# Reading the moving operand of float32r products as two interleaved halves

## The chip, the cores and the metric

One Trainium2 chip, one core. The metric is the device time of one launch in microseconds. TensorE, VectorE, ScalarE, GpSimd and SyncE appear in the profile as PE (with PEld for its weight loads), DVE, ACT, POOL and SP.

## What is computed

The reference, cut to what matters:

```python
x: (4, 12480, 128); inducing: (32, 128); w_in: (128, 2048); w_out: (2048, 128)
def mab(q, kv):
    s = scale * (q @ kv.transpose(0, 2, 1))
    a = softmax(s)
    return a @ kv
h   = mab(inducing for each batch, x)      # 32 summary rows per batch
y   = mab(x, h).reshape(49920, 128)        # every token attends to its batch's 32 rows
g   = y @ w_in
out = maximum(0.01 * g, g) @ w_out
```

All of it is float32.

## The kernel before

A token's attention output is `a @ h`, with `a` 32 wide, so the kernel never forms it: for each batch it makes `hw = h @ w_in` once (32 x 2048) and multiplies the 32-wide weights `a` by that. The leaky part is split as `0.99 * relu(g) + 0.01 * g`. The second half is linear and becomes one more 32-row product (`linear_part`, and the `LINEAR` branch of `products`), so that the main work is relu and two products.

Tokens are taken in tiles of 512 columns (`TOK`); two tiles are 384 wide, put together from two batches' remainders of 192. Every tile goes through 16 slices `f` of the hidden dimension. To keep float32 accuracy at the speed of float32r, each operand is split into a high and a low float32r part, and a product is three passes: high times high, low times high, high times low.

For one tile and slice:
- the first product, three passes with 32 contracted rows (`quarter`, L1147 to 1151, operands `A4` and `hw`), into a PSUM bank `ph`;
- the split of relu(`ph`) into `ghi` and `glo`. On the near way ACT writes `ghi` (`high`, L1135) and DVE takes `max(ph, 0) - ghi` as `glo` (`low`, L1138). On the far way ACT copies relu(`ph`) to `g` in SBUF, and POOL makes `ghi` (L1417, or L1111) and `glo` (L1419, or L1113) from it. POOL has no part in PSUM here;
- the second product, with 128 contracted rows. In the main part it is cut into four groups of 32 rows of the array that run side by side: each row group makes its three passes of 32 rows into its own bank, again through `quarter`. So a tile and slice costs 3 + 4 x 3 = 15 quarter passes, and four quarter passes run at once in the four row groups. Only the first two tiles and the last use the whole array for the second product (`ffn_second`, L1180).

After slice 15 the four banks of a tile are gathered: ACT copies banks 0 and 2 to SBUF (`copied`, L1445), DVE adds banks 1 and 3 (`summed`, L1451), POOL adds the two sums (`joined`, L1462), DVE transposes blocks (`store`, L1205) and SP sends the result out. The three tiles with one bank are transposed straight from PSUM.

The order of all instructions on all engines is written out when the program is built. A planner in the kernel (`turn_over`, `option`, `go`, `relu`, `best`, `clustered`) keeps a clock for each engine and each row group and issues next what can start first by these clocks. Its costs are constants: `QUARTER` for a 512-column pass, `RELU`, `LOW`, `FAR_HIGH`, `FAR_LOW` and so on for the other steps (`spent`, `on_rows`, `on_array`), and `SLOT` for the pace of a tile and slice, by which `relu` decides for the far way only if POOL would be done in time. The attention work of later batches (L395, L482, L575, L817) runs between the products in gangs that `clustered` lets in, held back by `IDLE`, `HURRY`, `WAITING` and the list `WAITS`. The engines keep semaphores between them, so a wrong clock makes a wait and not a wrong result.

The moving operand of every product above is read in order, one column after the other, from SBUF:

```python
nc.tensor.matmul(dst, w[32 * r : 32 * r + 32], x[32 * r : 32 * r + 32], ...)
```

Of the kernel before, what the change touches and what calls it, by code (L numbers as in the profile page):

```python
# [9 lines left out]
F32 = mybir.dt.float32  # L10
# [9 lines left out]
def induced_attention_then_leaky_ffn(  # L20
# [34 lines left out]
    while N - base >= 4 * TOK:  # L55
# [29 lines left out]
    A4_BUFS = 3  # L85
    XR = 7
    GB = 10
    SLOT = 868.0
    QUARTER = 232.6
    SIGNAL, TO_ARRAY, TO_POOL = 35.0, 150.0, 160.0  # L90
    DRAINED = 200.0
    TURNED, LOADED = 100.0, 100.0
    LANDED = 3800.0
    RELU, LOW, COPIED, ADDED, BLOCKS = 599.0, 690.0, 587.0, 691.0, 702.0
    FAR_HIGH, FAR_LOW, FAR_SUM = 613.0, 1310.0, 1297.0
    SETTLED = 75.0
    EARLY, PREFER, YIELDING, PATIENCE = 250.0, 0.0, 200.0, 6000.0
    IDLE, HURRY, APART, TAIL, WAITING, SOON = 600.0, 3000.0, 60000.0, 5000.0, 3000.0, 3000.0
    NEAR, BANKS, AT_ONCE, BEHIND = 3, 1, 2000.0, 1200.0
    LINEAR = NF - 3  # L100
    SPREAD = 80.0
    BEGUN = 3
    WAITS = [
# [3 lines left out]
    ]  # L107
    AHEAD = 100.0
    PACE, STOCK = 41250.0, 4
# [35 lines left out]
    def spent(engine, ns, *after):  # L145
        if not timing[0]:
            return 0.0
        signal = TO_POOL if engine == POOL else SIGNAL
        clock[engine] = max([clock[engine], now[0], *(a + signal for a in after)]) + ns
        return clock[engine]  # L150

    def on_array(kind, ns, *after):
        if not timing[0]:
# [943 lines left out]
    def split_first(ph, t, f, at):  # L1097

        _, n = spans(t)
        ghi = sb.tile([P, TOK], F32R, tag="ghi", name="ghi", bufs=GB)  # L1100
        glo = sb.tile([P, TOK], F32R, tag="glo", name="glo", bufs=GB)
        live[t, f] = (ghi, glo)
        start = max(clock[ACT], at + SIGNAL)
        if far_ends[-2:-1] <= [start] and max(clock[POOL], start + RELU) + FAR_HIGH + FAR_LOW < (
            max(clock[DVE], start + RELU) + LOW + BEHIND
        ):
            g = sb.tile([P, TOK], F32, tag="g", name="g", bufs=2)
            high(ph, g, n)
            at = spent(ACT, RELU, at)
            done(ph, at)  # L1110
            nc.gpsimd.tensor_copy(ghi[:, :n], g[:, :n])  # L1111
            high_of[t, f] = spent(POOL, FAR_HIGH, at)
            nc.gpsimd.tensor_tensor(  # L1113
                out=glo[:, :n], in0=g[:, :n], in1=ghi[:, :n].bitcast(F32), op=ALU.subtract
            )
            low_of[t, f] = spent(POOL, FAR_LOW) + SETTLED
            far_ends.append(low_of[t, f])
            return
        high(ph, ghi, n)
        high_of[t, f] = at = spent(ACT, RELU, at)  # L1120
        low(ph, ghi, glo, n)
        low_of[t, f] = at = spent(DVE, LOW, at)
        done(ph, at)
# [9 lines left out]
        return start + ns + DRAINED  # L1133

    def high(ph, ghi, n):  # L1135
        nc.scalar.activation(ghi[:, :n], ph[:, :n], AF.Relu)  # L1136

    def low(ph, ghi, glo, n):  # L1138
        nc.vector.scalar_tensor_tensor(  # L1139
            out=glo[:, :n],  # L1140
            in0=ph[:, :n],
            scalar=0.0,
            in1=ghi[:, :n].bitcast(F32),
            op0=ALU.max,
            op1=ALU.subtract,
        )

    def quarter(dst, w, x, r, start, stop):
        nc.tensor.matmul(  # L1149
            dst, w[32 * r : 32 * r + 32], x[32 * r : 32 * r + 32],  # L1150
            start=start, stop=stop, tile_position=(32 * r, 0),
        )

# [7 lines left out]
    def ffn_first(t, f):  # L1161

        n = spans(t)[1]
        ph = gen_ps("ph")
        for o, w, wt, a, k in first_products(t, f):
            quarter(ph[:, o : o + w], wt, a, f % 4, k == 0, k == 2)
            at = on_rows(f % 4, QUARTER * w / TOK, max(rows[f % 4], landed.get(("A", t), 0.0) + SIGNAL))
            if o + w == n:
                yield
        split_first(ph, t, f, at)  # L1170

    def ffn_second(t, f):

        parts, n = spans(t)
        ghi, glo = live.pop((t, f))
        if f == 0:
            accs[t] = bank("out")
        po = accs[t]
        for w, r in ((w_hi, ghi), (w_lo, ghi), (w_hi, glo)):
            nc.tensor.matmul(  # L1180
                po[:, :n], w[:, f, :], r[:, :n], start=(f == 0 and r is ghi and w is w_hi),
                stop=(t > 0 and f == NF - 1 and r is glo),
            )
            at = on_array("f", QUARTER * n / TOK, (high_of if r is ghi else low_of)[t, f])
        return at

    def linear_part(t):

        parts, n = spans(t)
        for b, o, w in parts:  # L1190
            for k in range(3):
                nc.tensor.matmul(
                    accs[t][:, o : o + w], hw[b][1 + k % 2][:M, TOK:], A4[t][:M, k // 2, o : o + w],
                    start=False, stop=(t == 0 and k == 2 and o + w == n), tile_position=(0, 0),
                )
                at = on_array("r", QUARTER * w / TOK)
        del A4[t]
        landed["A4"] = at
        return at

    def store(t, total, summed, at=0.0):
        _, n = spans(t)
        yield from new(DVE, at)
        osb = sb.tile([P, TOK], F32, tag="osb", name="osb", bufs=2)
        nc.vector.transpose(osb[:, :n], total[:, :n])  # L1205
        at = spent(DVE, BLOCKS, at)
        if summed:
            parts_used[0] -= 1
        else:
            done(total, at)  # L1210
        yield from old(HEAVY)
        o = 0
        for b, g, js in tiles[t]:
            base, J, K = GROUPS[g]
            n = 32 * K
            for j in js:
                yield from new(SP, at)
                row = b * N + base + j * 32 * K
                dst = out[row : row + n, :].rearrange("(r k) c -> r k c", k=K)
                for cb in range(NB):  # L1220

                    (nc.scalar if t == NT - 1 and cb % 2 else nc.sync).dma_start(
                        dst[:, :, 32 * cb : 32 * cb + 32],
                        osb[32 * cb : 32 * cb + 32, o : o + n].rearrange("p (k c) -> p k c", c=32),
                    )
                    spent(SP, 675.0, at)
                o += n
            yield from old()
# [40 lines left out]
    with tc.manual_schedule():  # L1269
# [131 lines left out]
        def relu(i, ph, ready):  # L1401
# [7 lines left out]
            if far_open[0] < 2 and left <= start and far <= wanted:  # L1409
                g = sb.tile([P, TOK], F32, tag="g", name="g", bufs=2)  # L1410
                high(ph, g, n)
                at = spent(ACT, RELU, ready)
                done(ph, at)
                far_open[0] += 1

                def on_pool():
                    nc.gpsimd.tensor_copy(ghi[:, :n], g[:, :n])  # L1417
                    high_at[i] = spent(POOL, FAR_HIGH, at)
                    nc.gpsimd.tensor_tensor(  # L1419
                        out=glo[:, :n], in0=g[:, :n], in1=ghi[:, :n].bitcast(F32), op=ALU.subtract  # L1420
                    )
                    low_at[i] = spent(POOL, FAR_LOW) + SETTLED
                    far_ends.append(low_at[i])
                    far_open[0] -= 1

                add(POOL, at, FAR_HIGH + FAR_LOW, on_pool)
                return
# [10 lines left out]
        def gather(t, r, ready):  # L1438
# [3 lines left out]
            def copied():  # L1442
                parts_used[0] += r == 0
                part = sb.tile([P, TOK], F32, tag="part", name="part", bufs=2)
                nc.scalar.copy(part[:, :n], po[:, :n])  # L1445
                parts_of[t, r] = part, spent(ACT, COPIED, ready)
                done(po, clock[ACT])

            def summed():
                part, at = parts_of[t, r - 1]  # L1450
                nc.vector.tensor_tensor(out=part[:, :n], in0=po[:, :n], in1=part[:, :n], op=ALU.add)  # L1451
                at = spent(DVE, ADDED, ready, at)
                parts_of[t, r] = part, at
                done(po, at)
                if r == 3:
                    add(POOL, at, FAR_SUM, joined, lambda: (t, 1) in parts_of)
# [70 lines left out]
        def go(r, kind, start):  # L1527
# [12 lines left out]
            if kind == "on":  # L1540
# [2 lines left out]
                _, n = spans(t)  # L1543
                o, w, wt, a, k = todo.pop(0)
                quarter(ph[:, o : o + w], wt, a, r, k == 0, k == 2)
                at = on_rows(r, QUARTER * w / TOK, start)
                if not todo:
                    running_first[r] = None
                    add(ACT, at, RELU, lambda: relu(i, ph, at))
# [10 lines left out]
                accs[t, r][:, o : o + width], w, x, r,  # L1560
                f == 0 and product_of[r] == 0, f == NF - 1 and last,
            )
            at = on_rows(r, QUARTER * width / TOK, start)
            product_of[r] += 1
            if last:
                product_of[r] = 0
# [169 lines left out]
```

## Time and profile before

| | us |
|---|---|
| median of 3 runs (1524.4 to 1525.05) | 1524.87 |
| span of the profiled execution, first to last instruction | 1523.1 |
| median less that span | 1.77 |
| PE busy / POOL busy | 1508.4 / 1363.5 |
| ACT busy / DVE busy | 1072.7 / 1029.2 |

Busy time is the time in which at least one instruction of the engine ran. Matmuls overlap, so a busy PE says only that it never stood still. The tables by line give, after the count, the group's busy time in us and the mean duration in ns of one instruction. In tables by stage every engine has its busy time and, in brackets, its count of instructions.

### The profile page before, as it was taken

Reading aid. Unit: us, or ns where it says so; the run is one execution under the profiler, and the core shown is the slowest. Engines: PE = TensorE matmul, PEld = TensorE weight load, DVE = VectorE, ACT = ScalarE, POOL = GpSimd, SP = SyncE. Lnnn points to the kernel's source line nnn. Section 1 sums busy time; section 2 is a strip of 40 time slices with the busy share of each in tenths; the row PEclk is TensorE's granted clock in tenths of the full one; section 3 lists DMA queues with packets and bytes.
Section 4 is the critical chain, followed back from the end, with each engine's and each line's share of the span. In section 5 each row is a group of like instructions: output and inputs, shape, how many; then the busy total and the mean of one; then the engine's idle time right before and its main releaser. Section 6 shows DMA issues by size and latency. Waiting matters only on the chain.

```text
span 1523.1 us, 60527 instructions
## 1 busy us (share of the span) xinstructions
PE 1508.4 (99%) x25207; PEld 1347.1 (88%) x25207; DVE 1029.2 (68%) x1811; ACT 1072.7 (70%) x1956; POOL 1363.5 (90%) x1435
## 2 busy tenths in 40 slices
PE   8999999999999999999999999999999999999998
PEld 5689989888899989888989999888899889999997
DVE  6867777666677777666677677666667666576564
ACT  6566777766777677776767777677777777777774
POOL 1478999999999999889989998999999999989997
PEclk9999999999999999999999999999999999999999
DMA  8155555443544454442644445342223223223231
GB/s 280 17 123 95 98 100 111 88 101 87 96 79 92 77 114 85 94 106 65 117 79 86 83 101 106 85 99 58 51 57 64 51 57 61 51 55 66 53 63 22
DMA packets 400706, 128.52 MB, mean 84 GB/s; under 512 B 373136, under 2 KB 375600, under 8 KB 400432
## 3 DMA queue, kind: packets, MB, share of 16 engines
q1 hardware_dynamic: 399328, 124.50, 39.3%
q8 instruction: 198, 3.24, 0.9%
q14 instruction: 76, 0.62, 0.1%
q10 hardware_dynamic: 1104, 0.15, 0.1%
HBM read 48.94 MB, written 25.56 MB: 49 GB/s over the span
## 4 chain that ended last, share of the span: by engine, by line
PE 97%; DVE 1%; ACT 1%; DMA 0%; issue 0%; POOL 0%; SPq 0%; DVEq 0%; ACTq 0%; POOLq 0%
PE bank L1149 89%; PE bank L395 3%; PE bank L1180 2%; PE bank L575 2%; PE bank L722 1%; DMA xr<-in_x_dram 0%; DVE glo L1139 0%; ACT xT L728 0%; ACT ghi L1136 0%; PE bank L817 0%; DVE cv_t L227 0%; PE bank L1055 0%; DVE sm L950 0%; SPq L700 0%; PE bank L482 0%
## 5 line engine op out<-in xcount | busy, mean ns | idle before, releaser
L1149 PE MATMUL bank<-ghi,w_hi 32*128 32x512 f32 (+1 forms) x6080 | 1182.5, 390 | 0.0
L1149 PE MATMUL bank<-ghi,w_lo 32*128 32x512 f32 (+1 forms) x6080 | 1180.4, 389 | 0.0
L1149 PE MATMUL bank<-glo,w_hi 32*128 32x512 f32 (+1 forms) x6080 | 1178.3, 389 | 0.0
L1149 PE MATMUL bank<-A,hwhi 32*128 32x512 f32 (+1 forms) x3394 | 1016.4, 387 | 0.2
L1139 DVE SCALAR_TENSOR_TENSOR glo<-bank,ghi 128x512 fp32r<-128x512 f32 (+1 forms) x948 | 632.1, 682 | 371.8 <-ACT ghi L1136 354.0
L1419 POOL TENSOR_TENSOR glo<-g,ghi 128x512 fp32r<-128x512 f32 (+1 forms) x611 | 789.0, 1291 | 48.9
L1149 PEld LDWEIGHTS bank<-ghi,w_hi 32*128 32x128 f32 x6080 | 757.2, 183 | 25.7 <-issue 1.4
L1149 PEld LDWEIGHTS bank<-ghi,w_lo 32*128 32x128 f32 x6080 | 752.8, 183 | 24.1 <-issue 1.6
L1149 PEld LDWEIGHTS bank<-glo,w_hi 32*128 32x128 f32 x6080 | 752.1, 183 | 24.1 <-issue 2.2
L1136 ACT ACTIVATE ghi<-bank 128x512 fp32r<-128x512 f32 (+1 forms) x948 | 552.9, 597 | 160.4 <-PE bank L1149 135.3
L1149 PE MATMUL bank<-A,hwlo 32*128 32x512 f32 (+1 forms) x1697 | 606.0, 385 | 0.0
L1149 PEld LDWEIGHTS bank<-A,hwhi 32*128 32x128 f32 x3394 | 552.3, 183 | 19.2 <-issue 2.4
L1136 ACT ACTIVATE g<-bank 128x512 f32<-128x512 f32 (+1 forms) x620 | 370.0, 598 | 217.8 <-PE bank L1149 194.1
L1417 POOL CAST ghi<-g 128x512 fp32r<-128x512 f32 (+1 forms) x611 | 374.0, 612 | 36.9 <-ACT g L1136 28.8
L1149 PEld LDWEIGHTS bank<-A,hwlo 32*128 32x128 f32 x1697 | 297.3, 183 | 6.4 <-issue 0.8
L1451 DVE TENSOR_TENSOR part<-bank,part 128x512 f32<-128x512 f32 (+1 forms) x190 | 129.8, 684 | 57.3 <-PE bank L1149 29.4
L1462 POOL TENSOR_TENSOR part<-part 128x512 f32<-128x512 f32 (+1 forms) x95 | 122.8, 1293 | 0.8 <-DVE part L1451 0.8
L1445 ACT COPY part<-bank 128x512 f32<-128x512 f32 (+1 forms) x190 | 110.9, 584 | 15.4 <-PE bank L1149 8.8
L1205 DVE STREAM_TRANSPOSE osb<-part 128x512 f32<-128x512 f32 (+1 forms) x95 | 66.8, 703 | 14.3 <-POOL part L1462 12.6
L531 DVE STREAM_TRANSPOSE xT<-xc 128x512 f32<-128x512 f32 x72 | 46.4, 682 | 0.0
L452 ACT ACTIVATE e<-e,nm 128x512 f32<-128x512 f32 (+1 forms) x28 | 18.7, 668 | 19.7 <-DVE least L440 19.3
L993 POOL TENSOR_TENSOR both<-aT,both 128x512 fp32r<-128x512 f32 x24 | 31.8, 1326 | 0.0
(135 smaller groups left out, 649.3 us busy)
## 6 DMA issues: line engine op xcount, KB each, us to landing
A<-both SPq DMA_DIRECT2D x376, 128.0 KB, 2.4
xr<-in_x_dram SPq DMA_DIRECT2D x96, 256.0 KB, 4.3
out_dram<-osb SPq DMA_DIRECT2D x382, 64.0 KB, 2.2
xc<-in_x_dram SPq DMA_DIRECT2D x288, 64.0 KB, 2.8
raw<-in_moe_w_in_dram SPq DMA_DIRECT2D x4, 512.0 KB, 6.8
raw<-in_moe_w_out_dram SPq DMA_DIRECT2D x4, 512.0 KB, 7.8
A<-both SPq DMA_DIRECT2D x48, 16.0 KB, 1.8
out_dram<-osb SPq DMA_DIRECT2D x48, 8.0 KB, 1.8
```

The lines of the kernel that those rows point to most:

```text
L395: nc.tensor.matmul(dst, lhsT, rhs, start=True, stop=True)
L531: nc.vector.transpose(t[:, j, :], blk.rearrange("p n c -> p (n c)"))
L993: (eng or nc.gpsimd).tensor_tensor(out=alo[sl], in0=aT.pop((b, g))[: 32 * J, :], in1=ahi[sl].bitcast(F32), op=ALU.subtract,)
L1136: nc.scalar.activation(ghi[:, :n], ph[:, :n], AF.Relu)
L1139: nc.vector.scalar_tensor_tensor(out=glo[:, :n], in0=ph[:, :n], scalar=0.0, in1=ghi[:, :n].bitcast(F32), op0=ALU.max, op1=ALU.subtract,)
L1149: nc.tensor.matmul(dst, w[32 * r : 32 * r + 32], x[32 * r : 32 * r + 32], start=start, stop=stop, tile_position=(32 * r, 0),)
L1205: nc.vector.transpose(osb[:, :n], total[:, :n])
L1417: nc.gpsimd.tensor_copy(ghi[:, :n], g[:, :n])
L1419: nc.gpsimd.tensor_tensor(out=glo[:, :n], in0=g[:, :n], in1=ghi[:, :n].bitcast(F32), op=ALU.subtract)
L1445: nc.scalar.copy(part[:, :n], po[:, :n])
L1451: nc.vector.tensor_tensor(out=part[:, :n], in0=po[:, :n], in1=part[:, :n], op=ALU.add)
L1462: nc.gpsimd.tensor_tensor(out=total[:, :n], in0=total[:, :n], in1=part[:, :n], op=ALU.add)
```

## The change

Three things. First, `woven` gives the moving operand of every 512-column product as columns 0, 256, 1, 257, ... of the SBUF tile, so that output column 2i + j of the bank belongs to column 256j + i of the operand. Passes of another width stay as they are. Second, whoever reads a 512-column bank (`high`, `low`, `copied`, `summed`, and `store` for the three tiles without a sum) puts the columns back: `unwoven` reads the bank by steps of two, first the even columns, then the odd, and writes SBUF in order. `store` makes two transposes of 256 columns there in place of one of 512. The steps on POOL read SBUF and stay. Third, the planner's constants change: a woven pass counts 216, another 232.6 per 512 columns; an engine's clock is set back by `OVERLAP` after each step; POOL's second far step gets `CHAINED` on top; and `SLOT`, `IDLE`, `HURRY`, `WAITING` and `WAITS` have new values.

```diff
-    SLOT = 868.0
-    QUARTER = 232.6
+    SLOT = 800.0
+    QUARTER, PLAIN = 216.0, 232.6
+    OVERLAP = {ACT: 95.0, DVE: 75.0, POOL: 55.0, SP: 0.0}
+    CHAINED = 135.0
-    RELU, LOW, COPIED, ADDED, BLOCKS = 599.0, 690.0, 587.0, 691.0, 702.0
-    FAR_HIGH, FAR_LOW, FAR_SUM = 613.0, 1310.0, 1297.0
+    RELU, LOW, COPIED, ADDED, BLOCKS = 599.0, 691.0, 587.0, 691.0, 702.0
+    FAR_HIGH, FAR_LOW, FAR_SUM = 613.0, 1297.0, 1299.0
-    IDLE, HURRY, APART, TAIL, WAITING, SOON = 600.0, 3000.0, 60000.0, 5000.0, 3000.0, 3000.0
+    IDLE, HURRY, APART, TAIL, WAITING, SOON = 1300.0, 1000.0, 60000.0, 5000.0, 3500.0, 3000.0
...
-        clock[engine] = max([clock[engine], now[0], *(a + signal for a in after)]) + ns
-        return clock[engine]
+        end = max([clock[engine], now[0], *(a + signal for a in after)]) + ns
+        clock[engine] = end - OVERLAP[engine]
+        return end
...
     def high(ph, ghi, n):
-        nc.scalar.activation(ghi[:, :n], ph[:, :n], AF.Relu)
+        ph, ghi = unwoven(ph[:, :n], ghi[:, :n])
+        nc.scalar.activation(ghi, ph, AF.Relu)
 
     def low(ph, ghi, glo, n):
+        ph, ghi, glo = unwoven(ph[:, :n], ghi[:, :n].bitcast(F32), glo[:, :n])
...
+    def woven(x):
+        n = x.shape[1]
+        return x.rearrange("p (j i) -> p i j", j=2) if n == TOK else x
+
+    def unwoven(ps, *flat):
+        if ps.shape[1] != TOK:
+            return (ps, *flat)
+        return (
+            ps.rearrange("p (i j) -> p j i", j=2),
+            *(f.rearrange("p (j i) -> p j i", j=2) for f in flat),
+        )
+
+    def pass_time(n):
+        return QUARTER if n == TOK else PLAIN * n / TOK
+
     def quarter(dst, w, x, r, start, stop):
         nc.tensor.matmul(
-            dst, w[32 * r : 32 * r + 32], x[32 * r : 32 * r + 32],
+            dst, w[32 * r : 32 * r + 32], woven(x[32 * r : 32 * r + 32]),
...
-                po[:, :n], w[:, f, :], r[:, :n], start=(f == 0 and r is ghi and w is w_hi),
+                po[:, :n], w[:, f, :], woven(r[:, :n]), start=(f == 0 and r is ghi and w is w_hi),
...
-        nc.vector.transpose(osb[:, :n], total[:, :n])
+        if summed or n != TOK:
+            nc.vector.transpose(osb[:, :n], total[:, :n])
+        else:
+            got, put = unwoven(total[:, :n], osb[:, :n])
+            for j in range(2):
+                nc.vector.transpose(put[:, j], got[:, j])
...
-                nc.scalar.copy(part[:, :n], po[:, :n])
+                got, put = unwoven(po[:, :n], part[:, :n])
+                nc.scalar.copy(put, got)
...
-                nc.vector.tensor_tensor(out=part[:, :n], in0=po[:, :n], in1=part[:, :n], op=ALU.add)
+                got, put = unwoven(po[:, :n], part[:, :n])
+                nc.vector.tensor_tensor(out=put, in0=got, in1=put, op=ALU.add)
```

## Rows read from the trace of the kernel before

**Rows 1.** The page: the span and the engines' busy time.

```profile
span 1523.1 us, 60527 instructions
...
PE 1508.4 (99%) x25207; PEld 1347.1 (88%) x25207; DVE 1029.2 (68%) x1811; ACT 1072.7 (70%) x1956; POOL 1363.5 (90%) x1435
```

**Rows 2.** The chain that ended last: shares of the span by line.

```profile
by line: PE bank L1149 88.9%; PE bank L395 3.0%; PE bank L1180 1.5%; PE bank L575 1.5%; PE bank L722 0.7%; DMA xr<-in_x_dram 0.4%; DVE glo L1139 0.4%; issue 0.3%; ACT xT L728 0.3%; ACT ghi L1136 0.2%; PE bank L817 0.2%; DVE cv_t L227 0.1%; 
```

**Rows 3.** Busy time by stage, all engines: stage, length, engines, PEclk, DMA share, GB/s.

```profile
0.00:92.00 92.00, 82.27 (x744) 55.65 (x745) 67.54 (x172) 53.30 (x110) 32.99 (x35) 0.98 0.45 136
200.00:1400.00 1200.00, 1199.86 (x20800) 1079.53 (x20796) 814.80 (x1390) 861.81 (x1564) 1122.29 (x1182) 1.00 0.40 82
1400.00:1480.00 80.00, 80.00 (x1383) 79.94 (x1379) 46.81 (x71) 58.55 (x104) 77.04 (x82) 1.00 0.29 59
```

**Rows 4.** PE by line and shape, 1400 to 1480 us.

```profile
L1149 PE MATMUL bank<-ghi,w_hi 32*128 32x512 f32 x364 | 67.9, 390 | 0.0
L1149 PE MATMUL bank<-ghi,w_lo 32*128 32x512 f32 x364 | 67.7, 390 | 0.0
...
L1149 PE MATMUL bank<-A,hwhi 32*128 32x512 f32 x194 | 62.1, 389 | 0.0
L1149 PE MATMUL bank<-A,hwlo 32*128 32x512 f32 x97 | 35.9, 389 | 0.0
```

**Rows 5.** PE in order of time, whole-array passes: start, duration (us).

```profile
58.35 0.39 PE L1180 MATMUL bank<-ghi,w_hi 128*128 128x512 f32 x1
58.58 0.39 PE L1180 MATMUL bank<-ghi,w_lo 128*128 128x512 f32 x1
58.81 0.40 PE L1180 MATMUL bank<-glo,w_hi 128*128 128x512 f32 x1
```

**Rows 6.** PE by line and shape, 92 to 1510 us.

```profile
L1149 PE MATMUL bank<-ghi,w_hi 32*128 32x512 f32 x5952 | 1163.5, 391 | 0.0
L1149 PE MATMUL bank<-ghi,w_lo 32*128 32x512 f32 x5952 | 1161.5, 390 | 0.0
...
L1149 PE MATMUL bank<-A,hwhi 32*128 32x512 f32 x3180 | 986.7, 390 | 0.1
L1149 PE MATMUL bank<-A,hwlo 32*128 32x512 f32 x1590 | 585.7, 390 | 0.0
```

**Rows 7.** Line 1149 alone, 92 to 1510 us: PE, PEld, PEclk, DMA share, GB/s.

```profile
92.00:1510.00 1418.00, 1354.15 (x23214) 1251.05 (x23214) 1.00 0.40 81
```

**Rows 8.** Weight loads beside the passes, whole kernel.

```profile
L1149 PEld LDWEIGHTS bank<-ghi,w_hi 32*128 32x128 f32 x6080 | 757.2, 183 | 25.7 <-issue 1.4 <-DVE hacc L592 0.7 <-ACT both L986 0.4
```

**Rows 9.** By line and shape, whole kernel: the steps that read the banks, and POOL's.

```profile
L1419 POOL TENSOR_TENSOR glo<-g,ghi 128x512 fp32r<-128x512 f32 x600 | 777.8, 1296 | 48.0
...
L1139 DVE SCALAR_TENSOR_TENSOR glo<-bank,ghi 128x512 fp32r<-128x512 f32 x927 | 620.8, 685 | 364.2 <-ACT ghi L1136 347.8 <-POOL ghi L1417 5.4 <-POOL glo L1419 1.3
...
L1136 ACT ACTIVATE ghi<-bank 128x512 fp32r<-128x512 f32 x927 | 542.6, 599 | 156.7 <-PE bank L1149 132.2 <-DVE osb L1205 1.5 <-DVE xT L531 0.7
L1417 POOL CAST ghi<-g 128x512 fp32r<-128x512 f32 x600 | 368.4, 614 | 34.0 <-ACT g L1136 27.9 <-PE bank L1149 5.4 <-DMA xc<-in_x_dram 0.2
L1136 ACT ACTIVATE g<-bank 128x512 f32<-128x512 f32 x609 | 364.6, 599 | 211.7 <-PE bank L1149 188.4 <-POOL ghi L1417 12.4 <-POOL glo L1419 3.5
...
L1451 DVE TENSOR_TENSOR part<-bank,part 128x512 f32<-128x512 f32 x186 | 127.6, 686 | 56.5 <-PE bank L1149 29.4 <-ACT part L1445 24.5 <-ACT hwhi L802 0.9
...
L1445 ACT COPY part<-bank 128x512 f32<-128x512 f32 x186 | 109.0, 587 | 15.2 <-PE bank L1149 8.6 <-DVE hacc L592 2.5
```

**Rows 10.** By line and shape, 0 to 57 us: SBUF reads, L208, L213 by steps of two.

```profile
L208 ACT ACTIVATE cv_a<-raw 128x512 f32<-128x512 f32 x6 | 4.1, 680 | 0.0
L223 DVE TENSOR_SCALAR cv_b<-cv_a 128x512 int32<-128x512 int32 x6 | 2.6, 426 | 0.2
...
L213 DVE TENSOR_SCALAR cv_b<-raw 128x512 int32<-128x512 int32 x6 | 2.5, 418 | 0.0
...
L283 ACT CAST w_hi<-wraw 128x512 fp32r<-128x512 f32 x2 | 1.2, 622 | 0.0
```

More of the change, by code (lines that the diff above doesn't have):

```diff
@@ L1115, in split_first @@
             )
-            low_of[t, f] = spent(POOL, FAR_LOW) + SETTLED
+            low_of[t, f] = spent(POOL, CHAINED + FAR_LOW) + SETTLED
             far_ends.append(low_of[t, f])
@@ L1135, in high @@
     def high(ph, ghi, n):
-        nc.scalar.activation(ghi[:, :n], ph[:, :n], AF.Relu)
+        ph, ghi = unwoven(ph[:, :n], ghi[:, :n])
+        nc.scalar.activation(ghi, ph, AF.Relu)
     def low(ph, ghi, glo, n):
+        ph, ghi, glo = unwoven(ph[:, :n], ghi[:, :n].bitcast(F32), glo[:, :n])
         nc.vector.scalar_tensor_tensor(
-            out=glo[:, :n],
-            in0=ph[:, :n],
+            out=glo,
+            in0=ph,
             scalar=0.0,
-            in1=ghi[:, :n].bitcast(F32),
+            in1=ghi,
             op0=ALU.max,
@@ L1166, in ffn_first @@
             quarter(ph[:, o : o + w], wt, a, f % 4, k == 0, k == 2)
-            at = on_rows(f % 4, QUARTER * w / TOK, max(rows[f % 4], landed.get(("A", t), 0.0) + SIGNAL))
+            at = on_rows(f % 4, pass_time(w), max(rows[f % 4], landed.get(("A", t), 0.0) + SIGNAL))
             if o + w == n:
@@ L1180, in ffn_second @@
             nc.tensor.matmul(
-                po[:, :n], w[:, f, :], r[:, :n], start=(f == 0 and r is ghi and w is w_hi),
+                po[:, :n], w[:, f, :], woven(r[:, :n]), start=(f == 0 and r is ghi and w is w_hi),
                 stop=(t > 0 and f == NF - 1 and r is glo),
             )
-            at = on_array("f", QUARTER * n / TOK, (high_of if r is ghi else low_of)[t, f])
+            at = on_array("f", pass_time(n), (high_of if r is ghi else low_of)[t, f])
         return at
@@ L1192, in linear_part @@
                 nc.tensor.matmul(
-                    accs[t][:, o : o + w], hw[b][1 + k % 2][:M, TOK:], A4[t][:M, k // 2, o : o + w],
+                    accs[t][:, o : o + w], hw[b][1 + k % 2][:M, TOK:],
+                    woven(A4[t][:M, k // 2, o : o + w]),
                     start=False, stop=(t == 0 and k == 2 and o + w == n), tile_position=(0, 0),
                 )
-                at = on_array("r", QUARTER * w / TOK)
+                at = on_array("r", pass_time(w))
         del A4[t]
@@ L1421, in on_pool @@
                     )
-                    low_at[i] = spent(POOL, FAR_LOW) + SETTLED
+                    low_at[i] = spent(POOL, CHAINED + FAR_LOW) + SETTLED
                     far_ends.append(low_at[i])
@@ L1545, in go @@
                 quarter(ph[:, o : o + w], wt, a, r, k == 0, k == 2)
-                at = on_rows(r, QUARTER * w / TOK, start)
+                at = on_rows(r, pass_time(w), start)
                 if not todo:
@@ L1562, in go @@
             )
-            at = on_rows(r, QUARTER * width / TOK, start)
+            at = on_rows(r, pass_time(width), start)
             product_of[r] += 1
```

6 rows, old and new, of the table WAITS are left out of this document.

## The prediction

> **What bounds the kernel now.** I begin with the page's list of engines [rows 1]: PE is busy for 99% of the span, POOL for 90%, ACT for 70%, DVE for 68%. PE is the candidate, but a busy PE need not be a fast one, so the chain that ended last comes next [rows 2]: 88.9% of the span lies on line 1149, the quarter passes; the attention's products on PE add about 5%, and no line of another engine holds half a per cent. The table by stage [rows 3] says where this holds. From 200 to 1400 us PE stands still for 0.14 us of 1200; only the first 92 us, where weights are converted, leave it idle. PEclk there is 1.00: the clock is at its 2.4 GHz level all the time, so no clock is to be won back.
>
> How long is one pass? The durations of about 390 ns [rows 4] are those of overlapping instructions and are no pace. From 1400 to 1480 us every matmul is a 512-column pass of line 1149: 364 for each of the three second products (two are shown), 194 and 97 for the first, together the 1383 of that stage [rows 3, 4]. Four run side by side, so a pass takes 80 us x 4 / 1383 = 231.4 ns. At 2.4 GHz 512 columns are 213.3 ns. The excess of 18.1 ns is what the change can win. It does not come from four row groups in each other's way: whole-array passes, one at a time, start every 0.23 us too [rows 5].
>
> **The change, part by part.** *Passes.* After 92 us there are 3 x 5952 + 3180 + 1590 = 22626 woven quarter passes (the third second product, with the same count, is not shown) [rows 6], that is 5656.5 rounds of four, and the last tile adds 16 slices x 3 = 48 whole-array passes: 5704.5 passes in a row on the path. The 96 whole-array passes of the first two tiles lie in the first 92 us beside the weights' conversion, and I cost them at nothing (1.5 us at 15.4 ns each, were that cover gone).
>
> No row shows a moving operand read with a jump between columns. The low end is the clock, 213.3 ns. The high end is open: nothing excludes that a jump of 256 columns costs more than reading in order. I take 216, the figure that the changed planner itself counts. This is an assumption, not a measurement; I lean to it because the excess shows in both ways of tiling and so goes with the operand's stream, the one thing that weaving alters. The gain is (231.4 - 216) x 5704.5 = 87.8 us; at the clock bound it would be 103.2 us. Weight loads don't forbid it: one takes 183 ns beside the pass before it [rows 8], 33 less than 216.
>
> The Trainium skill, TensorE: Matmul & The Clock Gate, section on the 56 ns gap, has warm 512-column matmuls start every 215.7 ns. The trace does not agree for these float32r passes read in order (231.4); if weaving brought them to that page's pace, an estimate of the gain would be 89.6 us.
>
> *Reading the banks by steps of two.* No row shows this either; the nearest are SBUF reads by steps of two in the start-up [rows 10]. On DVE they cost nothing (418 ns against 426 in order). On ACT the stepped read took 680 against 622, 58 ns more, though the two are not quite the same operation. So bounds of 0 and 58 for ACT, 0 for DVE by these rows. At 58 ns the 927 + 609 + 186 reads of ACT [rows 9] add 100 us of busy time, 1173 of about 1437, or 82%: still off the path. The path cost is 0 at either end, since up to ten split slices (`GB`) stand ready for PE, and DVE now idles 348 us waiting for ACT in `low` [rows 9]. That cover is gone only when ACT is full, at (1437 - 1073) / 1722 = 211 ns more per read.
>
> *POOL.* Its steps don't change, but its time does. In the stage from 200 to 1400 us it is busy for 1122.3 us [rows 3], 93.5%. The gain shortens that stage by about 1200 x 87.8 / 1418 = 74 us, to 1126, which POOL's present work would fill to 99.7%. A far slice costs POOL 614 + 1296 = 1.91 us, the near way DVE 0.685 us [rows 9]. To keep POOL at 93.5% (1053 us) some 37 slices must go near, 25 us more for DVE: 840 of 1126, 75%; ACT comes to 77%. There is room, and `relu` sends a slice far only if POOL will be done in time by its clock. Path cost: 0.
>
> *Store.* For three tiles two half transposes replace one. Only the last tile's is on the path, between 0 and one more DVE step of 0.69 us [rows 9]; I take 0.3.
>
> *The planner.* `OVERLAP`, `CHAINED` and the rest move no data; they change the order. PE doesn't wait now, so they can win only what lies between passes: line 1149 holds PE for 1354.2 us [rows 7], of which the woven passes are 5656.5 x 231.4 = 1308.9 and the 588 narrower passes at most 588 / 4 x 173.6 = 25.5. The other 20 us are changes of tiling and irregular passes. I take 0, with -10 and +15 as bounds: the loss is larger because with every engine fuller each late slice costs PE directly.
>
> **Sum.** 1523.1 - 87.8 + 0.3 = 1435.6 us of span, and 1.8 us around it, as the median stands now over the profiled span: **1437 us**. Its own range is 1421 (pass at the clock bound) to 1452 (new waits of 15 us).
>
> **Rivals.**
>
> *POOL becomes the bound.* The far share stays because the planner's clock for POOL is optimistic (it is set back 55 ns per step), and slices come late from POOL. For it: 93.5% now, the highest after PE. Against it: the far way is chosen by a test of time, and `CHAINED` adds 135 ns there. If POOL stops at 96.5%, the stage takes 1122.3 / 0.965 = 1163 us and saves 37 in place of 74: about 1474 us.
>
> *Weaving does nothing.* The 18.1 ns may lie between two passes and not in the reading order; rows at one width can't tell these apart. Then the pass stays at 231.4 while the plan counts 216. The order stays valid, and POOL and DVE finish as before: 1525 us, or 1520 to 1540 with a worse order.
>
> *Weaving costs.* Each column now comes from another place than the one before it, and if the read pays for the jump, every woven pass grows. It decides from 231.4 ns on, and each ns is 5.7 us. Priced by ACT's stepped read, 680 / 622 = 1.093 [rows 10], a pass is 253 ns and the time 1525 + 21.5 x 5.7045 = 1648 us; at one column per cycle of the 1.2 GHz level (426.7 ns) it would be about 2640. For it: the ACT rows. Against it: DVE's rows show no such cost, and no row has TensorE doing this.
>
> The Trainium skill, Advanced Engine Details and Errata, section Memory Cachelines, backs this rival: SBUF gives full speed while accesses stay in a 16-byte line, wants at least two hits on a line, and charges for a new line each time, and PSUM has 8-byte lines. By that rule the weave, with a new line per column, is the wrong way round. No run here shows it for TensorE; the DVE rows speak against it, the ACT rows for it.
>
> **How the numbers follow.** About 0.2%, 3 us, is what a measurement of this kernel can tell from no change. The forecast gets 0.76, POOL as the bound 0.08, no effect 0.06 (half of it within 0.2%, a third slower, a sixth faster), a costly weave 0.10. That makes faster 0.85, same 0.03, slower 0.12. The range from 1421 to 1468 holds the forecast with its bounds and the milder part of the POOL case; the rest, and the two cases without a gain, are the 2 in 10 left out.
>
> **What would show it.** In a stage with nothing but quarter passes, 80 us should hold about 1480 of them, not 1383, and whole-array passes should start every 0.215 us. The mean duration on line 1149 should fall from 390 to about 375 ns. ACT's `ghi` should stay between 599 and 657 ns, DVE's `glo` at 685. POOL's far count should fall from 600 to some 560 at a like share of the span. PE should still be busy all the time between 200 us and the end. If the passes shorten and PE shows idle time before L1149, POOL or ACT took over; if they stay at 231 ns, the excess was never in the reading order; if they are longer, the jump costs.

## The result, and the profile after

The changed kernel takes 1436.97 us (median of 4 runs, 1436.48 to 1438.54) against 1524.67 us for the kernel before on the same chip: a ratio of 0.943, 95% interval 0.941 to 0.944. The profiled execution has a span of 1434.7 us.

The page of the changed kernel: span, and busy time by engine, to be held against [rows 1].

```profile
span 1434.7 us, 60214 instructions
...
PE 1418.0 (99%) x25207; PEld 1301.2 (91%) x25207; DVE 1070.6 (75%) x1913; ACT 1066.0 (74%) x1956; POOL 1178.9 (82%) x1237
```

PE has the same 25207 matmuls and lost 90 us of busy time, about as much as the span (88 us). POOL lost 185 us and 198 instructions; DVE took over 41 us. PE is still what the chain lies on, against [rows 2]:

```profile
by line: PE bank L1171 86.5%; PE bank L398 3.0%; PE bank L578 1.6%; PE bank L1202 1.3%; DVE glo L1144 0.8%; PE bank L725 0.7%; issue 0.6%; DMA xr<-in_x_dram 0.6%; ACT ghi L1140 0.4%; DMA out_dram<-osb 0.2%; PE bank L820 0.2%; SPq L1012 0.2%
```

The table by stage (stage, length, then PE, PEld, DVE, ACT, POOL busy and their counts, PEclk, DMA share, GB/s), against [rows 3]:

```profile
0.00:92.00 92.00, 81.74 (x753) 57.62 (x755) 68.01 (x175) 53.63 (x110) 31.89 (x34) 0.98 0.46 138
200.00:1320.00 1120.00, 1118.54 (x20679) 1036.73 (x20675) 848.99 (x1472) 852.05 (x1557) 947.23 (x995) 1.00 0.43 88
1320.00:1400.00 80.00, 80.00 (x1481) 79.58 (x1477) 53.03 (x81) 62.48 (x110) 75.53 (x80) 1.00 0.31 63
```

In the last row 80 us hold 1481 quarter passes where 1383 stood before. By the same count a pass is 80 x 4 / 1481 = 216.1 ns, against 231.4. The first 92 us hardly moved (753 matmuls against 744), and the clock stands where it stood. (A pass by count takes in the passes that overlap the ends of the stage, so it is good to about half a per cent.)

PE in order of time, whole-array passes of the changed kernel (start, duration in us), against [rows 5]:

```profile
58.01 0.38 PE L1202 MATMUL bank<-ghi,w_hi 128*128 128x512 f32 x1
58.22 0.38 PE L1202 MATMUL bank<-ghi,w_lo 128*128 128x512 f32 x1
58.44 0.38 PE L1202 MATMUL bank<-glo,w_hi 128*128 128x512 f32 x1
58.65 0.38 PE L1202 MATMUL bank<-ghi,w_hi 128*128 128x512 f32 x1
```

They start every 0.21 to 0.22 us in place of 0.23: the pass is shorter in both ways of tiling.

By line and shape, whole changed kernel: a group of passes, the reads of the banks, and POOL's far steps, against [rows 6, 9].

```profile
L1171 PE MATMUL bank<-ghi,w_hi 32*128 32x512 f32 x5952 | 1147.2, 376 | 0.2
...
L1144 DVE SCALAR_TENSOR_TENSOR glo<-bank,ghi 128x512 fp32r<-128x512 f32 x1024 | 674.8, 684 | 248.6 <-ACT ghi L1140 236.2 <-POOL ghi L1445 3.7 <-POOL glo L1447 0.9
L1447 POOL TENSOR_TENSOR glo<-g,ghi 128x512 fp32r<-128x512 f32 x504 | 646.8, 1283 | 40.4
L1140 ACT ACTIVATE ghi<-bank 128x512 fp32r<-128x512 f32 x1024 | 596.8, 600 | 146.5 <-PE bank L1171 124.1 <-POOL glo L1447 2.3 <-DVE glo L1144 1.0
...
L1140 ACT ACTIVATE g<-bank 128x512 f32<-128x512 f32 x512 | 306.8, 599 | 143.2 <-PE bank L1171 85.3 <-POOL ghi L1445 18.6 <-POOL glo L1447 5.4
...
L1481 DVE TENSOR_TENSOR part<-bank,part 128x512 f32<-128x512 f32 x186 | 127.8, 688 | 58.8 <-PE bank L1171 37.5 <-ACT part L1474 10.6 <-ACT ghi L1140 6.9
...
L1474 ACT COPY part<-bank 128x512 f32<-128x512 f32 x186 | 108.8, 586 | 12.3 <-PE bank L1171 10.5
```

Reading a bank by steps of two costs nothing that can be told from the rows: ACT 600 and 599 ns (599 before), DVE 684 (685) and 688 (686), the copy 586 (587). The far slices of full width went from 609 to 512 (504 here and 8 on another line; before, 600 and 9).

### The profile page after: what moved, and what is told of

The parts are those of the page before. It is cut to its first block, busy times and chain, and to the rows that moved or that the text cites. A ratio compares the mean times of both kernels' runs of the same rounds, so it can differ in the third digit from the quotient of the medians.

```text
span 1434.7 us, 60214 instructions
## 1 busy us (share of the span) xinstructions
PE 1418.0 (99%) x25207; PEld 1301.2 (91%) x25207; DVE 1070.6 (75%) x1913; ACT 1066.0 (74%) x1956; POOL 1178.9 (82%) x1237
## 4 chain that ended last, share of the span: by engine, by line
PE 94%; DVE 2%; ACT 1%; DMA 1%; issue 1%; POOL 1%; SPq 1%; DVEq 0%; ACTq 0%; POOLq 0%
PE bank L1171 87%; PE bank L398 3%; PE bank L578 2%; PE bank L1202 1%; DVE glo L1144 1%; PE bank L725 1%; DMA xr<-in_x_dram 1%; ACT ghi L1140 0%; DMA out_dram<-osb 0%; PE bank L820 0%; SPq L1012 0%; ACT xT L731 0%; POOL glo L1447 0%; PE bank L1058 0%; SPq L703 0%
## 5 line engine op out<-in xcount | busy, mean ns | idle before, releaser
L1171 PE MATMUL bank<-A,hwhi 32*128 32x512 f32 (+1 forms) x3394 | 993.6, 373 | 0.8 <-DVE glo L1144 0.4
L1144 DVE SCALAR_TENSOR_TENSOR glo<-bank,ghi 128x512 fp32r<-128x512 f32 (+1 forms) x1047 | 687.2, 681 | 254.1 <-ACT ghi L1140 241.4
L1171 PEld LDWEIGHTS bank<-ghi,w_hi 32*128 32x128 f32 x6080 | 805.1, 184 | 16.5 <-issue 2.7
L1171 PEld LDWEIGHTS bank<-ghi,w_lo 32*128 32x128 f32 x6080 | 807.0, 184 | 12.4 <-issue 2.0
L1171 PEld LDWEIGHTS bank<-glo,w_hi 32*128 32x128 f32 x6080 | 806.8, 184 | 11.8 <-issue 1.0
L1140 ACT ACTIVATE ghi<-bank 128x512 fp32r<-128x512 f32 (+1 forms) x1047 | 608.0, 597 | 151.3 <-PE bank L1171 128.4
L1447 POOL TENSOR_TENSOR glo<-g,ghi 128x512 fp32r<-128x512 f32 (+1 forms) x513 | 656.0, 1279 | 41.1
L1140 ACT ACTIVATE g<-bank 128x512 f32<-128x512 f32 (+1 forms) x521 | 311.2, 598 | 146.7 <-PE bank L1171 87.5
L1445 POOL CAST ghi<-g 128x512 fp32r<-128x512 f32 (+1 forms) x513 | 312.9, 610 | 106.5 <-ACT g L1140 80.0
L936 POOL TENSOR_TENSOR y<-y,mx 128x512 f32<-128x512 f32 (+1 forms) x24 | 24.4, 1018 | 9.6 <-DVE mx L932 8.3
```

The source lines that it names most:

```text
L1140: nc.scalar.activation(ghi, ph, AF.Relu)
L1144: nc.vector.scalar_tensor_tensor(out=glo, in0=ph, scalar=0.0, in1=ghi, op0=ALU.max, op1=ALU.subtract,)
L1171: nc.tensor.matmul(dst, w[32 * r : 32 * r + 32], woven(x[32 * r : 32 * r + 32]), start=start, stop=stop, tile_position=(32 * r, 0),)
L1447: nc.gpsimd.tensor_tensor(out=glo[:, :n], in0=g[:, :n], in1=ghi[:, :n].bitcast(F32), op=ALU.subtract)
```

## The experiments

### Which part of the change makes the gain

**The weave with the old plan.** All planner constants of before, weave and stepped reads kept:

```diff
-    SLOT = 800.0
-    QUARTER, PLAIN = 216.0, 232.6
-    OVERLAP = {ACT: 95.0, DVE: 75.0, POOL: 55.0, SP: 0.0}
-    CHAINED = 135.0
+    SLOT = 868.0
+    QUARTER, PLAIN = 232.6, 232.6
+    OVERLAP = {ACT: 0.0, DVE: 0.0, POOL: 0.0, SP: 0.0}
+    CHAINED = 0.0
...
(RELU to WAITS as before)
```

> The weave and the stepped bank reads, with every planner constant of before. If the reading order alone makes the gain, a pass takes 216 ns here too and the time is 1437 to 1460 us, the upper end because the old plan thinks PE slow and asks POOL for some 620 far slices. If the new plan makes a part of the gain, the time lies between 1460 and 1500 us although the pass is 216 ns. If the pass depends on the plan, it stays near 231 ns and the time near 1525 us.

Measured: 1484.02 us, ratio 0.973 (0.972 to 0.975). Less than half of the gain: 41 us of 88. The chain that ended last, by line, the table by stage of this kernel, and a group of its passes:

```profile
by line: PE bank L1171 53.4%; POOL glo L1447 11.1%; issue 7.4%; POOL ghi L1445 6.8%; POOL part L1492 2.8%; PE bank L398 2.2%; DVE glo L1144 1.6%; PE bank L578 1.4%; POOL both L996 1.1%; ACT ghi L1140 1.0%; ACT g L1140 0.9%; PE bank L1202 0.
200.00:1320.00 1120.00, 1111.50 (x19980) 985.73 (x19976) 767.12 (x1339) 805.26 (x1500) 1066.29 (x1135) 1.00 0.41 84
L1171 PE MATMUL bank<-ghi,w_lo 32*128 32x512 f32 x5952 | 1097.9, 377 | 0.0
```

The passes are as short as in the changed kernel (377 ns on average; 376 in the changed kernel's row above, 390 in order [rows 6]). So it is not the pass that costs. POOL is on the chain, which it was not in [rows 2]: 22% of the span on its lines shown here. It is busy for 1066 of 1120 us, 95%. Who waited for whom, longest first (us in total, times, longest), shows where POOL holds others up:

```profile
DVE glo L1144 <- ACT ghi L1140: 311.6, 365, 2.6
ACT g L1140 <- POOL glo L1447: 133.1, 223, 1.6
...
PEld bank L1171 <- POOL glo L1447: 20.1, 43, 1.0
...
PEld bank L1171 <- ACT g L1140: 15.1, 41, 0.9
```

ACT can't copy the next relu to `g` until POOL has released one of its two buffers; the bank stays held, and PE's next first product waits for one (last row shown). And POOL's own `glo` comes late for the second products (the row before it). In the changed kernel ACT's wait is 5.4 us and the one for `glo` 0.2. The two waits of PE's weight loads come to 35 us over four row groups, and this kernel takes 47 us longer than the changed one; that POOL makes up all of it is not shown, and a run below speaks against it.

The PE column hides the loss. The stage of 1120 us shows PE busy for 1111.5 us, 99.2%, but holds 19980 matmuls where the changed kernel's holds 20679, 3.4% fewer. While one row group runs, PE counts as busy, and the other three may stand empty.

**The plan without the weave.** `woven` and `unwoven` return what they get, all constants new:

```diff
-        return x.rearrange("p (j i) -> p i j", j=2) if n == TOK else x
+        return x
```

> All planner constants of the changed kernel, operands and banks read in order. If the reading order makes the gain, the pass is 231.4 ns again and the time 1520 to 1540 us, since the plan counts 216 ns for it. If the new plan has a gain of its own, below 1515 us.

Measured: 1527.14 us, ratio 1.0017 (1.0007 to 1.0026). 80 us without anything but quarter passes:

```profile
1400.00:1480.00 80.00, 80.00 (x1378) 79.84 (x1375) 49.42 (x76) 58.66 (x104) 71.69 (x76) 1.00 0.30 61
```

That is 80 x 4 / 1378 = 232 ns a pass, the old one again. The new plan is worth nothing, or costs 2.5 us, by itself; together with the weave it is worth 1484.0 - 1437.0 = 47 us. So the parts can't be priced one by one and added: the weave alone gives 41 us, the plan alone nothing, both together 88.

**Half of the weave.** The second and linear products woven, first products and `ph` in order:

```diff
     def quarter(dst, w, x, r, start, stop, turn=lambda x: x):
-            dst, w[32 * r : 32 * r + 32], woven(x[32 * r : 32 * r + 32]),
+            dst, w[32 * r : 32 * r + 32], turn(x[32 * r : 32 * r + 32]),
...
-                f == 0 and product_of[r] == 0, f == NF - 1 and last,
+                f == 0 and product_of[r] == 0, f == NF - 1 and last, woven,
```

> The second and the linear products woven, the first products (3 of 15.19 quarter passes) and their banks in order. If the excess belongs to each pass's own reading, the mean pass is 216.1 + 0.198 x 15.3 = 219.1 ns and the time about 1454 us. If four row groups disturb one another's reading, in-order passes slow down their neighbours and the mean pass is above 222 ns, the time above 1470 us.

Measured: 1454.20 us, ratio 0.954 (0.953 to 0.955), as worked out for passes that each keep their own pace. A stage of 60 us with nothing but 512-column quarter passes, and a group of woven passes:

```profile
1120.00:1180.00 60.00, 60.00 (x1097) 58.28 (x1094) 48.32 (x79) 48.29 (x87) 41.45 (x43) 1.00 0.31 64
L1171 PE MATMUL bank<-ghi,w_hi 32*128 32x512 f32 x5952 | 1162.7, 376 | 0.0
```

The mean pass by count is 60 x 4 / 1097 = 218.8 ns, against 219.1 expected, and more than 222 if row groups disturbed one another; the woven passes keep their 376 ns. An in-order pass in one row group doesn't measurably slow woven ones beside it.

### What in the new plan matters

**CHAINED alone.**

```diff
-    CHAINED = 135.0
+    CHAINED = 0.0
```

> The changed kernel with CHAINED at 0. The far count on POOL fell from 620 to 521 where 37 were forecast. If CHAINED holds slices back from POOL, the far count rises to 560 or more and POOL's busy time to 1250 us or more; the time stays within 5 us of 1437, since POOL is not on the path, or rises by 10 to 40 us if POOL then becomes the bound. If CHAINED has no part in it, the count stays near 521.

Measured: 1472.48 us, ratio 0.966 (0.964 to 0.967). The count is 539 far slices, 18 more than in the changed kernel and short of the 560 expected, so `CHAINED` is not what sent nearly 100 slices to DVE. But 35 us are lost, which the expectation had only beside a count of 560 or more. The chain, the table by stage, and who waited for whom in this kernel:

```profile
by line: PE bank L1171 51.0%; POOL glo L1447 6.4%; POOL ghi L1445 3.6%; issue 2.8%; PE bank L398 1.5%; POOL part L1492 1.3%; DVE glo L1144 1.0%; PE bank L578 0.8%; PE bank L1202 0.7%; ACT g L1140 0.5%; ACT ghi L1140 0.4%; POOL y L958 0.4%; 
200.00:1320.00 1120.00, 1115.41 (x20142) 1011.06 (x20138) 814.21 (x1426) 818.65 (x1516) 935.87 (x987) 1.00 0.42 86
ACT g L1140 <- POOL glo L1447: 81.8, 135, 3.3
POOL part L1492 <- DVE part L1481: 56.5, 14, 11.7
```

ACT's wait is the one seen under the old plan. POOL is on the chain again, though busy for only 936 of 1120 us, 84%, as in the changed kernel (85%): slices come late from it without its being full. The last row shows one such delay: POOL stands up to 11.7 us before a sum that DVE has not finished. A reason that fits is the plan's clock. `OVERLAP` sets POOL's clock back by 55 ns at each step, and without `CHAINED` the plan takes POOL to be free earlier than it is: the second far step stands idle for 40.4 / 504 = 80 ns on average before it starts (the row of L1447 above), and 135 - 55 is 80. That a wrong order follows from this, and from it the 35 us, is argued from these numbers; no run takes the steps apart.

**SLOT alone.**

```diff
-    SLOT = 800.0
+    SLOT = 868.0
```

> The changed kernel with SLOT at 868 as before. If SLOT sets how many slices go to POOL, the far count rises from 521 to 560 or more; PE then waits for POOL and the time is 1442 to 1470 us, or stays at 1437 if POOL is still in time. If the faster pass alone sets it, count and time stay.

Measured: 1452.14 us, ratio 0.952 (0.951 to 0.954), with 582 far slices: `SLOT` governs the count. The chain and the stage:

```profile
by line: PE bank L1171 87.5%; PE bank L398 3.1%; PE bank L578 1.6%; PE bank L1202 1.5%; DVE glo L1144 0.8%; PE bank L725 0.6%; issue 0.5%; DMA xr<-in_x_dram 0.4%; ACT xT L731 0.3%; ACT ghi L1140 0.3%; POOL glo L1447 0.2%; PE bank L820 0.2%;
200.00:1320.00 1120.00, 1118.06 (x20397) 1034.87 (x20393) 812.04 (x1394) 840.14 (x1533) 1036.44 (x1099) 1.00 0.42 86
```

61 slices more go with 15 us more. PE makes 20397 matmuls in the stage against 20679, so here too row groups stand empty; but POOL holds 0.2% of the chain, and ACT's wait for its `glo` is 3.5 us. What keeps them empty is not settled.

**The pass time and SLOT alone, in the old plan, with the weave.**

```diff
-    SLOT = 868.0
-    QUARTER, PLAIN = 232.6, 232.6
+    SLOT = 800.0
+    QUARTER, PLAIN = 216.0, 232.6
```

> The weave with the planner of before, but with the pass at 216 ns (232.6 for other widths) and SLOT at 800. The old plan lost 47 us of the gain (1484 against 1437 us). If it lost them because it took TensorE to be slow and so asked POOL for too much, the far count falls from 620 to 560 or fewer and the time to 1437 to 1450 us. If the truth of POOL's own clock (OVERLAP, CHAINED) is what matters, the time stays at 1460 us or above.

Measured: 1483.51 us, ratio 0.973 (0.971 to 0.974). Same time as the old plan, but with POOL off the chain. The chain and the stage of the same length in this kernel:

```profile
by line: PE bank L1171 86.3%; PE bank L398 2.9%; PE bank L578 1.5%; PE bank L1202 1.3%; DMA xr<-in_x_dram 1.0%; DVE glo L1144 0.8%; issue 0.6%; DVE xT L534 0.6%; ACT ghi L1140 0.6%; DMA raw<-in_moe_w_in_dram 0.4%; PE bank L725 0.2%; PE bank
200.00:1320.00 1120.00, 1114.29 (x19968) 1024.52 (x19964) 866.78 (x1506) 816.44 (x1499) 764.44 (x798) 1.00 0.41 84
```

POOL is now busy for 764 us, 68%, with 413 far slices; the matmul count is as low as under the old plan. The first branch of the expectation fails: the count fell, and the time did not. The time is the one that the second branch gave, for the truth of POOL's own clock, but with POOL off the chain the run doesn't show that clock to be the cause. So taking the load off POOL doesn't bring the 47 us back. A reason that fits, and is not tested, is that with `OVERLAP` at 0 the plan takes each engine to be slower than it is, and with a fast PE on top gives POOL too little. What then keeps row groups empty (no single wait on PE is large) was not settled; `IDLE` and `WAITS`, which let the attention's gangs in, are old here too and were not tried alone.

### Which order of reading is fast

Here only the order of the columns on TensorE changes (and, in the first, the readers with it).

**Four parts in turn:** 0, 128, 256, 384, 1, ..., and banks read by steps of four.

```diff
-        return x.rearrange("p (j i) -> p i j", j=2) if n == TOK else x
+        return x.rearrange("p (j i) -> p i j", j=4) if n == TOK else x
...
-            ps.rearrange("p (i j) -> p j i", j=2),
+            ps.rearrange("p (i j) -> p j i", j=4),
```

> The changed kernel with four parts in turn (columns 0, 128, 256, 384, 1, ...) and banks read by steps of four. If it is enough that two neighbours don't follow one another, the pass is 216 ns as with halves and the time 1434 to 1442 us. If the number of streams matters, four places in turn cost more than two: a pass above 220 ns and a time above 1455 us. If stepped bank reads cost by the size of the step, ACT's ghi is above 620 ns or DVE's glo above 710.

Measured: 1788.28 us, ratio 1.173 (1.171 to 1.175). Stepped bank reads stayed free at a step of four too (ACT `ghi` 599 ns, DVE `glo` 687); all of the loss is on TensorE.

**Every second column, every fourth, pairs, and two places half as far apart**, with the plan of the changed kernel and banks read in order (the remarks behind # are mine):

```diff
-        return x.rearrange("p (j i) -> p i j", j=2) if n == TOK else x
+        return x.rearrange("p (i j) -> p j i", j=2) if n == TOK else x             # every second
+        return x.rearrange("p (i j) -> p j i", j=4) if n == TOK else x             # every fourth
+        return x.rearrange("p (j i k) -> p i j k", j=2, k=2) if n == TOK else x    # pairs
+        return x.rearrange("p (h j i) -> p h i j", h=2, j=2) if n == TOK else x    # 0, 128, 1, 129, ...
```

> The plan of the changed kernel; on TensorE alone each 512-column operand is read 0, 2, 4, ... then 1, 3, 5, ...; the banks are read in order, so that the columns of the output stand in another order than the reference's. If only an order that leaves the 16-byte line at each column helps, the pass stays near 231 ns; if it is enough that adjacent columns do not follow one another, it is 216 ns. By the page's rule on lines (two hits a line) it would not be slower than in order.

> As step2, with the order 0, 4, 8, ... in four rounds (the output's columns stand in another order than the reference's). Each column lies in another 16-byte line than the one before, 16 bytes on. If leaving the line at each column helps, 216 ns; if a new line costs (the page's rule), well above 231 ns; if it takes two places far apart, 231 ns.

> As step2, with the order 0, 1, 256, 257, 2, 3, ... (the output's columns stand in another order than the reference's). If adjacent columns in turn are what costs, half of the steps still are: 220 to 231 ns. If two places far apart are what helps, 216 ns.

> The plan of the changed kernel; on TensorE alone the order is 0, 128, 1, 129, ..., then 256, 384, 257, ...; banks read in order (the output's columns stand in another order than the reference's). Two places in turn, as in the weave, but 512 bytes apart and not 1024. If two places at any distance give the fast pass and four places (279 ns) were too many, the pass is 216 ns. If the distance is what matters, it is 231 ns or more, like the four parts.

Measured, one run each: 2824, 2873, 2145 and 1436.93 us. A stage of 60 us with 512-column quarter passes alone on PE, in the kernels with four parts, every second, every fourth, pairs, and two places 512 bytes apart, in this order (columns as above):

```profile
1300.00:1360.00 60.00, 60.00 (x872) 47.92 (x868) 36.91 (x63) 38.46 (x67) 32.05 (x34) 1.00 0.24 48
```

```profile
180.00:240.00 60.00, 60.00 (x536) 32.73 (x532) 23.59 (x43) 23.70 (x42) 27.32 (x30) 1.00 0.25 45
```

```profile
180.00:240.00 60.00, 60.00 (x524) 35.47 (x523) 23.11 (x43) 23.00 (x40) 27.52 (x30) 0.99 0.25 45
```

```profile
865.00:925.00 60.00, 60.00 (x722) 45.79 (x717) 28.97 (x44) 31.10 (x54) 37.70 (x39) 1.00 0.37 76
```

```profile
1105.00:1165.00 60.00, 60.00 (x1114) 56.67 (x1110) 48.74 (x79) 48.59 (x87) 41.25 (x42) 1.00 0.31 63
```

With 60 x 4 / count (good to about 1%; the first two rows from stages of 80 us; four parts come to 275 by this count, where the expectation of the last run has 279):

| order of the columns | a pass, ns |
|---|---|
| in order (before) | 231 |
| 0, 256, 1, 257, ... (the change) | 216 |
| 0, 128, 1, 129, ... | 215 |
| 0, 128, 256, 384, 1, ... | 275 |
| 0, 1, 256, 257, 2, ... | 332 |
| 0, 2, 4, ... | 448 |
| 0, 4, 8, ... | 458 |

The granted clock is 0.99 to 1.00 in all of these stages, so none of it is the clock. Two places in turn, each going on by one column, are fast at either distance. Four places are too many. Both simple readings that the expectations tried fall: it is not enough that adjacent columns don't follow one another (every second column would be fast, and is twice as slow), and a new 16-byte line at each column is not in itself a loss (the change has one at each column, and no order is clearly faster). Why pairs from the same two places take 332 ns is open: most of these orders change the step between neighbours, the number of places that take turns and the nesting of the access pattern at once, and no run takes these apart.

**Columns or passes.** Everything in order, 448 columns in most passes:

```diff
+        if x.shape[1] == TOK and not start:
+            dst, x = dst[:, :448], x[:, :448]
```

> The plan of the changed kernel, everything read in order; of each quarter product's three passes the second and third take 448 of the 512 columns, the last 64 columns lack those parts. If the excess over the clock grows with the columns, these passes take 448 x 231.4 / 512 = 202.5 ns; if it is 18.1 ns for each pass, 186.7 + 18.1 = 204.8 ns.

Measured: 1405.41 us, one run. Inconclusive. `start` is true only for the first pass into a bank, so nearly all passes of the second products lost their last 64 columns, and not two in three as the expectation says. The chain of this kernel has POOL on it again (2.9% of the span on its far steps), so passes wait for other engines, and a difference of 2.3 ns per pass can't be read from its stages. Whether the excess in order grows with the columns stays open.

## Why the prediction was right, point by point

**The pass.** 216 ns were taken, 216.1 counted. The term of 87.8 us is the whole result: the span fell by 88.4, the median by 87.7 with before's 1524.67. That the sum meets the median to 0.1 us is luck: one ns in the pass is 5.7 us, and the count of passes is no better than that. The value was an assumption, and the reason given for it was weak. That the excess shows in both tilings is confirmed, and it did depend on the order of reading. But the same reason would have spoken for pairs or for every second column, which are slower than in order by 101 and 217 ns. What made the forecast right here is the planner's own 216.

**Stepped bank reads.** The bounds were 0 and 58 ns for ACT, 0 for DVE; measured are 0 to 1 ns for ACT and -1 to 2 for DVE. The 58 ns of the start-up's stepped read by ACT [rows 10] don't carry over to the banks. PSUM reads by steps of two or four cost neither engine anything here.

**POOL.** The path cost of 0 is right, and so is the reason: far slices moved to DVE. The size was off. I forecast some 37 slices, at a like share of 93.5% for POOL; 99 moved (620 to 521), and POOL is busy for 85% of the stage from 200 to 1320 us. My step held the share fixed, where `relu` compares POOL's end with a due time at a pace of `SLOT`. With `SLOT` back at 868 there are 582, that is 38 fewer than before, close to the 37 that I had worked out, and the kernel takes 15 us longer. So the lower `SLOT`, which my step left out, moved the rest.

**The planner.** "I take 0, with -10 and +15 as bounds" is the step that failed as a statement about the parts. In the sum it is harmless, since the forecast was of both together. But the constants don't only win what lies between passes: without them 47 us of the 88 are gone. With all the old constants this looks like my rival "POOL becomes the bound", priced at 1474 and measured at 1484: POOL is on the chain and busy for 95% of the stage. Without `CHAINED` (1472) POOL is on the chain too, but at 84%, so it is lateness and not a full engine that costs. And with the old constants but the new pass time and `SLOT`, POOL is at 68% and off the chain, and the time is 1484 all the same. So that the new constants matter is shown; how much of the 47 us is POOL's is open. I named `CHAINED` as what speaks against the rival; the run bears out that it matters, but not through the count.

**Weaving does nothing** is out: 1527 without it, and 232 ns a pass again. **Weaving costs** did not happen, but its near neighbours show that it was a real case and priced too low: 275 to 458 ns a pass, against the 253 that I took from ACT's row. My second price, 426.7 ns, is near the two slowest orders, but at a granted clock of 0.99 to 1.00 and not at the 1.2 GHz level. The rule in the Trainium skill, Advanced Engine Details and Errata, section Memory Cachelines, is half borne out. Every fourth column, one hit on each 16-byte line, is slow (458 ns). But every second column has the two hits that the rule asks for and is as slow (448), and the weave, a new line each time, is as fast as any order tried (216). For float32r operands of TensorE the measurement decides.

**The store.** Six half transposes came, as said; the last tile's pair takes 0.78 us in place of one of 0.72, so the 0.3 us in the sum were nearer 0.1.

## What to carry to other kernels

An operand's reading order can be a knob on a matmul's pace: for float32r here there is a factor of two between the best and the worst, and no simple rule foretold which order gets which, so run the exact order. When a step on the bounding engine gets shorter, plan the order of the others again; here half of the gain was lost without it. Where an engine's work is tiled, count its instructions in a stage: a busy share of 99% hid 3.4% fewer matmuls here.

## What was not expected of the hardware

The moving operand in float32r takes 448 ns where every second column is read and 216 ns where two halves are read in turn, at a granted clock of 1.00 both times. Two places 512 bytes apart do as well as two at 1024 (215 and 216 ns), four places in turn cost 59 ns more per pass. ACT and DVE read PSUM by steps of two and of four at the time of reading in order (`ghi` 599 to 600, `glo` 684 to 687 ns).
